# One product of ones fewer at the start, and the last subtraction of the logits moved behind h in two turns

## The chip, the cores and the metric

The kernel runs on one core of one Trainium2 chip. The time is device microseconds of one execution; several executions give a median. A profile of one execution is taken beside them, with the core's span (first to last instruction) and each engine's instructions. The engines are TensorE (PE; its weight loads are PEld), VectorE (DVE), ScalarE (ACT), GpSimd (POOL) and SyncE (SP, which issues most DMAs).

## The reference, cut

```python
h  = x + A_ref(layernorm(x), wqkv, w_phi, wo)   # x: 1 x 2048 x 512
h2 = h + B_ref(layernorm(h), w1, b1, w2, b2)

def A_ref(x, wqkv, w_phi, wo):                  # 32 heads of 16
    q, k, v = split_heads(x @ wqkv)
    pq, pk = q @ w_phi, k @ w_phi               # per head
    phi_q = concat(softmax(pq), softmax(-pq))   # 32 features; phi_k the same from pk
    kv, z = phi_k^T @ v, sum over s of phi_k
    o = (phi_q @ kv) / (phi_q @ z + 1e-6)
    return merge_heads(o) @ wo

def B_ref(x, w1, b1, w2, b2):                   # across the 2048 tokens
    u = gelu(x^T @ w1 + b1)                     # 512 x 1792
    return (u @ w2 + b2)^T
```

## The kernel before, in words

The 2048 tokens are 16 tiles of 128 rows. Each float32 operand is split in a high and a low part, and a product is three matmuls: high by high, high by low, low by high (`mm3`, L64 to L68). The program has these stages:

- **Opening** (0 to about 45 us). `WARM` products of a 128x128 tile of ones (L352) run on TensorE before any weight has arrived. Then the weights of q and k are centred (`center`), folded with `w_phi` and a block pattern (`fold`, L330) and split.
- **Passes over the tiles** up to about 130 us: keys, values and the first query tiles. Here only TensorE's order is written by hand; the other engines' instructions are put in order by the program's own model of time.
- **Attention stage** (about 138 to 260 us): the loop `for it in range(NT + 2)`, 18 turns, with the order of TensorE, VectorE, ScalarE and GpSimd written by hand (`manual_schedule`): each of these engines does its instructions in the order in which the code issues them. A turn `it` holds steps for several tiles:
  - TensorE: `s_num(it-1)` (L609, tile `pn`), transposes `s_tr(it)` (L591), a first piece of `work` (half a projection of a query tile, `q_half`, or a step of the first w1 product, `fill`), `s_wo(it-1)` (`po`, L66 to L68), then the rest of `work`.
  - VectorE: the logits of a query tile, in three instructions: `mx` (L169), `mn` (L170) and the subtraction `eq<-pu,mx` (L163, `shift` in `logit_ops`), which reads the projection from PSUM; between the last two `ol` (L618); the two sums `smq` of another tile (L234, `q_sum`); the six instructions of `s_den` that end in the weights `w` (L497 to L505); `s_h` (L634: `h` = `po` + x, with its row sums), whose result SyncE stores; and low parts of w1 (`wlo`, L670, in `flush`).
  - GpSimd: `s_pq` (L508), `s_rstd` (L645), `s_ez` (L484), the low part of `hn` (L62) and `negate` (L177, L178), which makes the negated half of the logits that were subtracted a turn before.
  - ScalarE: moments of `h`, `oh` (L613), `pht` (L593), the exponentials (L189), `hn`, high parts of w1 (L663).
- **MLP**: the rest of the w1 products (`pu<-hs,whi`) up to about 376 us, then the w2 products (`py`).

Three things about PSUM matter here. The query projections `PS[t]` are tiles of the pool `ps_q`, which has two buffers used in turn. Once the logits of all 16 tiles have been issued, `fill(1, ps_q)` takes its two tiles from the same pool. `pn` and `po` share one buffer of the pool `ps_n`, which `oh`, `ol` and `h` read.

Which steps a turn holds follows from counters (`q["mm"]`, `q["logits"]`, `q["exp"]`, `q["sum"]`), the halves listed in `Q_TURNS`, and the rule that sums are taken only while `q["sum"] <= it + 2`. `ql` is the list of a turn's three logit steps, or empty; `sm` that of its two sums, or empty.

Of the kernel before, what the change touches and what calls it, by code (L numbers as in the profile page):

```python
# [29 lines left out]
SUMS = 8  # L30
Q_TURNS = ((0, 1), (0, 1), (0, 1), (0, 1), (0,), (1,), (0,), (1,))
LAG = 3
WARM = 10
EPS = 1e-5


# [1 line left out]
def block_kernel(ctx: ExitStack, tc: tile.TileContext, x, xT, wT, phic, wo, w1, b1, w2, b2,  # L38
# [134 lines left out]
    def negate():  # L173

        if MN:
            ev, mx, mn = MN.pop(0)
            nc.gpsimd.tensor_sub(mn, mn, mx)  # L177
            nc.gpsimd.tensor_sub(ev[:, :, 1], mn.unsqueeze(3).to_broadcast([P, NPR, 2, DH]), ev[:, :, 0])  # L178

    def turns(*lists):  # L180

        return [ops[i] for i in range(max(map(len, lists))) for ops in lists if i < len(ops)]

    def run(*lists):
        for op in turns(*lists):
            op()
# [56 lines left out]
    def q_logits(lag):  # L243
        n = q["logits"]
        if n < min(NT, q["mm"] - lag + NT * (q["mm"] == NT)):
            EQ[n] = big.tile([P, NG, P], F32, name="eq", tag="big")
            q["logits"] += 1
            return logit_ops(PS[n], EQ[n], n >= Q_EARLY)
        return []

    def q_exp(lag):
        n = q["exp"]
        if n < min(NT, q["logits"] - len(MN) - lag):
            exps(n, EQ[n])
            q["exp"] += 1

    def q_sums(lag):
        n = q["sum"]
        if n < min(NT, q["exp"] - lag + NT * (q["exp"] == NT)):
            q["sum"] += 1  # L260
            return q_sum(n)
        return []
# [12 lines left out]
    with tc.tile_pool(name="prep", bufs=1) as prep:  # L275
# [74 lines left out]
        warm = ps_k.tile([P, P], F32, name="pk_ps", tag="pk_ps")  # L350
        for _ in range(WARM):
            nc.tensor.matmul(warm, ones, ones, start=True, stop=True)  # L352
# [129 lines left out]
    def s_ez(t):  # L482
        EZ[t] = az.tile([P, NG, P], F32, name="ez")
        nc.gpsimd.tensor_mul(EZ[t], EQ[t], zB)  # L484
# [22 lines left out]
    def s_pq(t):  # L507
        nc.gpsimd.tensor_mul(heads(EQ[t]), heads(EQ[t]), W[t].rearrange("p g c h -> p (g c h)").unsqueeze(2).to_broadcast([P, 2 * H, DH]))  # L508
# [77 lines left out]
    def s_tr(t):  # L586
        PHT[t] = ak.tile([P, NG, P], F32, name="pht")
        ptr = ps_t.tile([P, 8, P], F32, name="tr").rearrange("p (r c) (a s) -> p r (c a) s", r=2, a=2)
        for g in range(NG):
            for r, rows in enumerate(HALF):  # L590
                nc.tensor.transpose(ptr[:, r, g, :], EQ[t][rows, g, :], ident[rows, rows])  # L591
        for r in range(2):
            nc.scalar.activation(PHT[t][:, :, r * 64:r * 64 + 64], ptr[:, r], AF.Copy)  # L593

    def s_kv():

        pt = banks("pt")[:, 0, 0:2]
        for b in range(2):
            nc.tensor.transpose(pt[:, b, :], kvS[:, 2 * b:2 * b + 2, :].rearrange("p n f -> p (n f)"), ident)
        nc.scalar.activation(kvB, pt, AF.Copy)  # L600

    def s_num(t):

        pn = banks("pn")[:, :, 0:2]
        for b in range(2):
            for c in range(4):
                for r, rows in enumerate(HALF):
                    cols = slice(32 * c, 32 * c + 32)
                    nc.tensor.matmul(pn[cols, r, b, :], kvB[rows, b, cols], PHT[t][rows, 4 * b + c, :],  # L609
                                     start=True, stop=True, skip_group_check=True)  # L610
        oh = ak.tile([P, 2, 2, P], F32R, name="oh")
        ol = ak.tile([P, 2, 2, P], F32R, name="ol")
        nc.scalar.activation(oh, pn, AF.Copy)  # L613
        OS[t] = oh, ol, pn

    def s_ol(t):
        oh, ol, pn = OS[t]
        return [lambda: nc.vector.tensor_sub(ol, pn, oh)]  # L618

    def s_wo(t):  # L620
        oh, ol, _ = OS.pop(t)
        PO[t] = po = banks("po")[:, 0].rearrange("p a s -> p (a s)")
        for j in range(4):
            mm3(po, oh[:, j // 2, j % 2, :], ol[:, j // 2, j % 2, :], woh[:, j, :], wol[:, j, :], j == 0, j == 3)

    def s_x(t):
        HT[t] = ak.tile([P, D], F32, name="h", bufs=4)
        nc.sync.dma_start(HT[t], x[t * P:(t + 1) * P, :])

    def s_h(t):  # L630

        h = HT[t]
        VE[t] = ak.tile([P, 4], F32, name="ve2", bufs=3)
        nc.vector.scalar_tensor_tensor(h, PO.pop(t), 1.0, h, op0=ALU.mult, op1=ALU.add, accum_out=VE[t][:, 2:3])  # L634
        nc.sync.dma_start(out[t * P:(t + 1) * P, :], h)

    def s_moments(t):

        junk = ak.tile([P, D], F32, name="hj", bufs=1)
        nc.scalar.activation(VE[t][:, 1:2], VE[t][:, 2:3], AF.Copy, scale=-1.0 / D)  # L640
        nc.scalar.activation(junk, HT[t], AF.Square, bias=VE[t][:, 1:2], accum_out=VE[t][:, 3:4])  # L641
        nc.scalar.activation(VE[t][:, 0:1], VE[t][:, 3:4], AF.Identity, scale=(1.0 + EPS) / D, bias=eps2)

    def s_rstd(t):
        nc.gpsimd.tensor_tensor(r2[:, t:t + 1], VE[t][:, 0:1], mhalf[:, :1], op=ALU.pow)  # L645

    def s_hn(t):
        hn = ak.tile([P, D], F32, name="hn")
        nc.scalar.activation(VE[t][:, 1:2], VE[t][:, 1:2], AF.Copy, scale=r2[:, t:t + 1])
        nc.scalar.activation(hn, HT[t], AF.Identity, scale=r2[:, t:t + 1], bias=VE[t][:, 1:2])  # L650
        HN[t] = big.tile([P, 2, D], F32R, name="hs", tag="big")
        split(HN[t][:, 0], HN[t][:, 1], hn, nc.gpsimd)
# [6 lines left out]
    def his():  # L659
        while COMING:  # L660
            LATER.append(COMING.pop(0))
            _, raw, wh_ = LATER[-1]
            nc.scalar.activation(wh_, raw, AF.Copy)  # L663

    def flush(n=None):
        if n is None:
            his()
        for _ in range(len(LATER) if n is None else min(n, len(LATER))):
            wl_, raw, wh_ = LATER.pop(0)
            LO.append(nc.vector.tensor_sub(wl_, raw, wh_).ins)  # L670
# [40 lines left out]
    def turn(it):  # L711

        halves = Q_TURNS[it] if it < len(Q_TURNS) else ()
        n = [FN[0] <= it - LAG and FN[0] < NT, min(2, max(0, it - LAG + 1 - FN[1])) if q["logits"] == NT else 0]
        for p in range(2):
            ahead = n[p] + 1 + p + 2 * (it == NT)
            if it >= (LAG - 1, len(Q_TURNS) - 1)[p] and FL[p] < min(NT, FN[p] + ahead):
                fill_load(p)
        return ([lambda i=i: q_half(i) for i in halves] + [lambda: fill(0, ps_f)] * n[0]
                + [lambda: fill(1, ps_q)] * n[1])  # L720

    for it in range(NT + 2):
        if it < NT:
            s_x(it)
        shifted = q["logits"] - len(MN)
        ql = q_logits(0)
        work = turn(it)
        if it > NT:
            his()
        if 0 <= it - 2 < NT:  # L730
            s_moments(it - 2)
        if 0 <= it - 1 < NT:
            s_num(it - 1)
        if it < NT:
            s_tr(it)
        if it + 1 < NT:
            s_pq(it + 1)
        for w in work[:1]:
            w()
        if it == 0:  # L740
            s_kv()
        if q["exp"] < shifted:
            q_exp(0)
        if 0 <= it - 2 < NT:
            s_rstd(it - 2)
        if it + 3 < NT:
            s_ez(it + 3)
        if 0 <= it - 2 < NT:
            s_hn(it - 2)
        negate()  # L750
        left = len(LATER)
        his()
        sm = q_sums(0) if q["sum"] <= it + 2 else []
        ol = s_ol(it - 1) if 0 <= it - 1 < NT else []
        run(ql[:2] + ol + ql[2:] if ql else sm[:1] + ol)
        flush(left)
        run(sm if ql else sm[1:])
        if it > 0 and it + 2 < NT:
            run(s_den(it + 2, ps_t, "tr"))
        if 0 <= it - 1 < NT:  # L760
            s_wo(it - 1)
        for w in work[1:]:
            w()
        if 0 <= it - 1 < NT:
            s_h(it - 1)
        flush(1)
    flush()
    ms.close()
# [306 lines left out]
```

## Time and profile before

| what | us |
|---|---|
| median of 3 runs | 519.4 (519.24 to 519.52) |
| the profiled execution | 519.69 |
| its span | 517.9 |
| TensorE busy | 513.2 |
| VectorE busy | 395.0 |
| ScalarE busy | 285.3 |
| GpSimd busy | 235.9 |

A busy time is the union of an engine's instructions. A line of an engine in order of time reads: start, length, engine, line, operation, what is written `<-` what is read, shapes, count, and in brackets idle time of the engine before it with what ended that. Matmuls overlap: the next one starts before the record of the last one ends, so the step from start to start is the measure. A line of the waits reads: who waited, for what, us in total, times, longest. In a line by stretches of time, the last three numbers are granted TensorE clock, DMA share and GB/s. 1.8 us of the profiled execution lie outside the span.

### The profile page before, as it was taken

The page shows a single profiled execution, that of the slowest core. Times are in us where ns is not written, and L with a number is a line of the kernel's source. Part 1 is how long each engine was busy: PE and PEld are TensorE (multiplying, and loading weights), DVE is VectorE, ACT ScalarE, POOL GpSimd, SP SyncE. Part 2 cuts the span into 40 slices and gives each one's busy share as a digit, 9 for nine tenths or more (in the row PEclk, how much of TensorE's full clock was granted, in tenths as well). Part 3 has the DMA queues.
Part 4 walks back from the last instruction along what each step waited for, and adds up shares of the span by engine and source line. Part 5 has one row for each costly group of instructions (what it writes and reads, how often), then busy time and mean ns, then how long its engine had stood idle before and what let it go on. Part 6 is the DMA issues. An engine that isn't in the chain of part 4 may idle for free.

```text
span 517.9 us, 9772 instructions
## 1 busy us (share of the span) xinstructions
PE 513.2 (99%) x3761; PEld 434.0 (84%) x3761; DVE 395.0 (76%) x719; ACT 285.3 (55%) x501; POOL 235.9 (46%) x182
## 2 busy tenths in 40 slices
PE   9999999999999999999999999999999999999997
PEld 8888888888887777777788888888899999999997
DVE  6799889989987899697336624625797899888993
ACT  6999853526267877767756423425464434433530
POOL 3579997876999999974224000000001102110210
PEclk9999999999999999999999999999999999999999
DMA  8642301021302334333255433532134586557732
GB/s 311 209 142 84 102 22 42 1 83 44 122 27 97 103 103 119 107 103 123 82 163 162 123 94 90 184 102 62 41 115 94 141 201 136 139 156 181 137 48 61
DMA packets 46493, 57.66 MB, mean 111 GB/s; under 512 B 4080, under 2 KB 33136, under 8 KB 46448
## 3 DMA queue, kind: packets, MB, share of 16 engines
q1 hardware_dynamic: 43136, 51.38, 31.4%
q0 software_dynamic: 3024, 5.51, 7.6%
q8 instruction: 29, 0.48, 0.4%
q10 hardware_dynamic: 288, 0.17, 0.1%
q14 instruction: 16, 0.13, 0.1%
HBM read 46.81 MB, written 10.22 MB: 110 GB/s over the span
## 4 chain that ended last, share of the span: by engine, by line
PE 97%; DVE 1%; ACT 1%; issue 0%; DVEq 0%
PE pu L66 13%; PE pu L68 12%; PE pu L67 12%; PE py L921 11%; PE py L913 10%; PE py L924 6%; PE po L66 3%; PE pk_ps L66 3%; PE po L68 3%; PE po L67 3%; PE pk_ps L67 3%; PE pk_ps L68 3%; PE pv L67 3%; PE pv L66 3%; PE pv L68 3%; PE tr L591 2%
## 5 line engine op out<-in xcount | busy, mean ns | idle before, releaser
L991 POOL DMA_DIRECT2D out<-ot x14 | 12.5, 941 | 170.3 <-DVE ot L972 170.3
L66 PE MATMUL pu<-hs,whi 128*128 128x512 f32 x224 | 87.7, 394 | 0.0
L67 PE MATMUL pu<-hs,whi 128*128 128x512 f32 x224 | 87.2, 389 | 0.0
L68 PE MATMUL pu<-hs,wlo 128*128 128x512 f32 x224 | 86.5, 389 | 0.0
L670 DVE TENSOR_TENSOR wlo<-wraw,whi 128x512 fp32r<-128x512 f32 x56 | 46.9, 841 | 46.5 <-ACT whi L663 46.2
L875 ACT ACTIVATE whi<-wraw 128x1792 fp32r<-128x1792 f32 x26 | 44.0, 1704 | 30.9 <-issue 17.4
L663 ACT ACTIVATE whi<-wraw 128x512 fp32r<-128x512 f32 x56 | 34.6, 625 | 44.4 <-PE pu L67 39.4
L875 DVE TENSOR_TENSOR wlo<-wraw,whi 128x1792 fp32r<-128x1792 f32 x26 | 52.4, 2019 | 0.0
L66 PEld LDWEIGHTS pu<-hs,whi 128*128 128x128 f32 x224 | 42.0, 188 | 9.1 <-ACT hj L641 0.2
L68 PEld LDWEIGHTS pu<-hs,wlo 128*128 128x128 f32 x224 | 42.0, 188 | 8.9
L67 PEld LDWEIGHTS pu<-hs,whi 128*128 128x128 f32 x224 | 42.1, 188 | 8.5
L921 PE MATMUL py<-uf,whi 128*128 128x512 f32 x175 | 48.4, 395 | 0.0
L484 POOL TENSOR_TENSOR ez<-eq,zB 128x1024 f32<-128x1024 f32 x16 | 38.4, 2405 | 3.8 <-ACT zB L544 3.8
L913 PE MATMUL py<-uf,whi 128*128 128x256 f32 x210 | 39.0, 283 | 0.0
L213 POOL TENSOR_TENSOR pk<-pk,sk 128x1024 f32<-128x1024 f32 x16 | 31.1, 1949 | 11.2 <-DVE sk L212 10.0
L508 POOL TENSOR_TENSOR eq<-eq,w 128x1024 f32<-128x1024 f32 x16 | 32.4, 2026 | 3.2 <-DVE w L505 3.2
L921 PEld LDWEIGHTS py<-uf,whi 128*128 128x128 f32 x175 | 30.1, 189 | 3.9
L913 PEld LDWEIGHTS py<-uf,whi 128*128 128x128 f32 x210 | 32.8, 192 | 0.0
L217 POOL TENSOR_TENSOR zacc<-zacc,pk 128x1024 f32<-128x1024 f32 x13 | 31.4, 2412 | 0.5
L924 PEld LDWEIGHTS py<-uf,wlo 128*128 128x128 f32 x175 | 27.1, 189 | 3.8
L913 PE MATMUL py<-uf,wlo 128*128 128x256 f32 x105 | 29.7, 283 | 0.0
L924 PE MATMUL py<-uf,wlo 128*128 128x256 f32 x175 | 28.7, 281 | 0.0
(200 smaller groups left out, 1303.9 us busy)
## 6 DMA issues: line engine op xcount, KB each, us to landing
wraw<-in_w SPq DMA_DIRECT2D x112, 256.0 KB, 3.0
xraw<-in_xT SPq DMA_DIRECT2D x16, 256.0 KB, 2.9
xh<-in_x SPq DMA_DIRECT2D x16, 256.0 KB, 2.6
h<-in_x SPq DMA_DIRECT2D x16, 256.0 KB, 2.7
out<-h SPq DMA_DIRECT2D x16, 256.0 KB, 2.1
out<-ot POOLq DMA_DIRECT2D x14, 256.0 KB, 4.4
wraw<-in_wT SPq DMA_DIRECT2D x12, 256.0 KB, 5.1
out<-low POOLq DMA_DIRECT2D x7, 256.0 KB, 4.2
```

The lines of the kernel that those rows point to most:

```text
L66: nc.tensor.matmul(o, ah, bh, start=first, stop=False)
L67: nc.tensor.matmul(o, ah, bl, start=False, stop=False)
L68: return nc.tensor.matmul(o, al, bh, start=False, stop=last).ins
L217: nc.gpsimd.tensor_add(zacc, zacc, PK[t])
L484: nc.gpsimd.tensor_mul(EZ[t], EQ[t], zB)
L508: nc.gpsimd.tensor_mul(heads(EQ[t]), heads(EQ[t]), W[t].rearrange("p g c h -> p (g c h)").unsqueeze(2).to_broadcast([P, 2 * H, DH]))
L663: nc.scalar.activation(wh_, raw, AF.Copy)
L670: LO.append(nc.vector.tensor_sub(wl_, raw, wh_).ins)
L875: in_order(lambda: nc.scalar.activation(wh_, raw, AF.Copy), lambda: nc.vector.tensor_sub(wl_, raw, wh_))
L913: in_order(lambda: nc.tensor.matmul(o, x[:, m[0]], UB[p, m[1]][:, y], start=opens and p == 0 and i == 0, stop=closes and p == NP - 1 and i ...
L921: in_order(lambda: nc.tensor.matmul(o, wh_[:, m[0]], UB[p, m[1]], start=p == 0, stop=False, skip_group_check=True))
L924: in_order(lambda: nc.tensor.matmul(o[:, 0], wl_[:, m[0]], UB[p, m[1]][:, 0], start=False, stop=p == NP - 1, skip_group_check=True))
```

## The change

`WARM` becomes 9 instead of 10. In the attention loop a turn that holds both logits and sums issues the last of its three logit steps (the subtraction L163, and the note for `negate` of the next turn) behind `s_h` instead of behind `ol`; other turns stay as they are.

```diff
-WARM = 10
+WARM = 9
...
         sm = q_sums(0) if q["sum"] <= it + 2 else []
         ol = s_ol(it - 1) if 0 <= it - 1 < NT else []
-        run(ql[:2] + ol + ql[2:] if ql else sm[:1] + ol)
+        late = ql[2:] if sm else []
+        run(ql[:2] + ol + (ql[2:] if not late else []) if ql else sm[:1] + ol)
         flush(left)
         run(sm if ql else sm[1:])
...
         for w in work[1:]:
             w()
         if 0 <= it - 1 < NT:
             s_h(it - 1)
+        run(late)
         flush(1)
```

## The prediction

> **What bounds the kernel now.** I read the page first, then the waits, then the stretch that the change touches, engine by engine in order of time.
>
> ```profile
> span 517.9 us, 9772 instructions
> PE 513.2 (99%) x3761; PEld 434.0 (84%) x3761; DVE 395.0 (76%) x719; ACT 285.3 (55%) x501; POOL 235.9 (46%) x182
> ...
> PE 97%; DVE 1%; ACT 1%; issue 0%; DVEq 0%
> ```
>
> The first two lines are the span and the busy times, the last is the chain that ended last. TensorE is busy in 513.2 of 517.9 us and makes up 97% of the chain. So the question for each edit is only this: when does the next matmul start? Work that another engine does sooner is worth nothing unless a matmul was waiting for it, and a new wait of TensorE is paid in full, since there is hardly an idle moment later on to take it back.
>
> The waits between 140 and 260 us (the attention stage) hold only these two of TensorE for VectorE (total, times, longest):
>
> ```profile
> PEld po L66 <- DVE ol L618: 0.9, 3, 0.4
> PE pn L609 <- DVE h L634: 0.2, 1, 0.2
> ```
>
> **Where the change acts.** In a turn the loop issues VectorE's work in a fixed order. The sums are taken only once tile `q["sum"]` is not above turn + 2, the logits only while tiles are left. Counting the four counters through the opening list of passes (six query tiles done there, ten projected before turn 0, the halves of `Q_TURNS` after) gives logits in turns 0 to 4, 6 and 8, and sums from turn 5 on. So `late` holds something in two turns, 6 (tile 14) and 8 (tile 15, the last). The trace agrees: a maximum `mx` and the sums `smq` stand in one turn only at 177 to 185 and at 193 to 200 us.
>
> **Turn 6, what is removed.** The two ends of the same step are VectorE's rows and TensorE's:
>
> ```profile
> 179.77 0.69 DVE L618 TENSOR_TENSOR ol<-pn,oh 128x512 fp32r<-128x512 f32 x1 [0.76 <-ACT oh L613]
> 180.37 0.68 DVE L163 TENSOR_TENSOR eq<-pu,mx 128x512 f32<-128x512 f32 x1
> 180.97 1.27 DVE L234 TENSOR_REDUCE smq<-eq 128x32 f32<-128x512 f32 x2
> ...
> 184.71 0.68 DVE L634 SCALAR_TENSOR_TENSOR h<-po,h 128x512 f32<-128x512 f32 x1
> ...
> 185.32 1.54 DVE L670 TENSOR_TENSOR wlo<-wraw,whi 128x512 fp32r<-128x512 f32 x1
> ```
>
> ```profile
> 178.04 0.39 PE L68 MATMUL pu<-hs,wlo 128*128 128x512 f32 x1
> 178.36 0.67 PE L609 MATMUL pn<-pht,kvB 64*32 64x128 f32 x32
> ...
> 183.58 0.39 PE L68 MATMUL po<-woh,ol 128*128 128x512 f32 x1
> ...
> 184.94 0.39 PE L68 MATMUL pu<-hs,wlo 128*128 128x512 f32 x1
> 185.55 0.67 PE L609 MATMUL pn<-pht,kvB 64*32 64x128 f32 x32 [0.22 <-DVE h L634]
> ```
>
> From 179.77 on VectorE never pauses; the subtraction `eq<-pu,mx` holds it for 0.60 us (180.37 to 180.97). `pn` of the next turn needs the bank that `h` reads. Its usual step behind the last matmul is 0.32 us (178.04 to 178.36); here it is 0.61. So `h` being late costs 0.29 us. With the subtraction behind it `h` starts at 184.11, its operand `po` being done by about 184.0 (183.58 plus 0.39). It ends 0.6 us sooner, and the wait of 0.29 us goes. Next to be late is nothing of VectorE's: `wlo` starts at 185.32 as before, since the same instructions have run without a pause.
>
> How much of the 0.29 lasts? Only as far as turn 8, where TensorE meets VectorE again. VectorE's own time gains less:
>
> ```profile
> 190.97 0.22 DVE L505 TENSOR_TENSOR w<-smq,tr 128x64 f32<-128x64 f32 x1
> 191.22 0.69 DVE L634 SCALAR_TENSOR_TENSOR h<-po,h 128x512 f32<-128x512 f32 x1
> ...
> 193.26 0.68 DVE L169 TENSOR_REDUCE mx<-pu 128x32 f32<-128x512 f32 x1
> ...
> 194.46 0.68 DVE L618 TENSOR_TENSOR ol<-pn,oh 128x512 fp32r<-128x512 f32 x1
> 195.06 0.68 DVE L163 TENSOR_TENSOR eq<-pu,mx 128x512 f32<-128x512 f32 x1
> 195.66 1.26 DVE L234 TENSOR_REDUCE smq<-eq 128x32 f32<-128x512 f32 x2
> ...
> 199.25 0.22 DVE L505 TENSOR_TENSOR w<-smq,tr 128x64 f32<-128x64 f32 x1
> 199.39 0.68 DVE L634 SCALAR_TENSOR_TENSOR h<-po,h 128x512 f32<-128x512 f32 x1
> ...
> 200.00 1.19 DVE L670 TENSOR_TENSOR wlo<-wraw,whi 128x512 fp32r<-128x512 f32 x1
> ```
>
> In turn 8, where VectorE is the late one, `h` follows 0.14 us behind the start of `w`; in turn 7 it is 0.25. TensorE coming sooner can save VectorE that 0.1 us and no more, after which all is back to back until 200 us.
>
> **Turn 8, what is added.** The subtraction also does something else: it is the last reader of the PSUM bank that holds tile 15's query projection. That pool (`ps_q`, two buffers) is handed on in turn: tile 14, tile 15, then the two `pu` tiles of the second pair of w1 columns, which `fill(1, ps_q)` opens in the first turn in which all 16 tiles have their logits. That is turn 8, the same turn, behind `po`:
>
> ```profile
> 195.19 0.49 PE L66 MATMUL po<-woh,oh 128*128 128x512 f32 x1
> 195.53 0.40 PE L67 MATMUL po<-wol,oh 128*128 128x512 f32 x1
> ...
> 197.80 0.39 PE L68 MATMUL po<-woh,ol 128*128 128x512 f32 x1
> 198.03 0.39 PE L66 MATMUL pu<-hs,whi 128*128 128x512 f32 x1
> ...
> 198.71 0.39 PE L66 MATMUL pu<-hs,whi 128*128 128x512 f32 x1
> 198.94 0.39 PE L67 MATMUL pu<-hs,whi 128*128 128x512 f32 x1
> ...
> 200.84 0.67 PE L609 MATMUL pn<-pht,kvB 64*32 64x128 f32 x32
> ```
>
> The three matmuls from 198.03 open the first of the two (tile 14's old bank, free since turn 6); those from 198.71 the second, in tile 15's bank. Before, that bank is free at 195.74 (195.06 plus 0.68), 3 us ahead. After, VectorE does sums and weights 0.60 us sooner, `h` at 198.79, and the subtraction 0.61 us behind it (199.39 to 200.00 is that step), at 199.40 to 200.08; less the 0.1 us of turn 7, 199.98. A weight load follows such an end by 0.05 us (`ol` ends at 195.14, `po` starts at 195.19), so the matmul of 198.71 starts at 200.03: 1.32 us later. Behind a wait the first step is 0.34 us (195.19 to 195.53) instead of 0.23 (198.71 to 198.94): 0.11 more. **Together 1.43 us**, which already contains turn 6's gain, because VectorE's time sets it and not TensorE's. Had only TensorE's earlier arrival counted, the 0.29 would be used up in the same wait.
>
> Queued behind the waiting load on TensorE are eight more matmuls of `fill(1)`, then `pn` and the transposes of turn 9; ScalarE's `oh`, VectorE's `ol` and the next `po` wait for `pn`. All of it moves by 1.43 us. From 200 us on only the two short waits for `ol` of the table above (under 0.9 us with the one at 195.19) could give some back: at most 0.2 us, taken as nothing. On the other engines the move costs nothing. VectorE: `wlo` behind it starts when it did before, and its weights are wanted turns later. GpSimd: the negated half is taken at 192.75 and 207.52 us, 7 us behind the subtraction. SyncE: the store of `h` is issued 0.6 us sooner, with no one behind it waiting.
>
> ```profile
> 192.75 0.70 POOL L177 TENSOR_TENSOR mn<-mn,mx 128x32 f32<-128x32 f32 x1
> ...
> 207.52 0.70 POOL L177 TENSOR_TENSOR mn<-mn,mx 128x32 f32<-128x32 f32 x1
> ```
>
> **The opening.** One product of ones is two matmul records (20 for ten).
>
> ```profile
> 4.54 0.78 DVE L322 TENSOR_SCALAR wraw<-wraw,mu 128x256 f32<-128x256 f32 x2
> ...
> 4.62 1.06 PE L352 MATMUL pk_ps<-ones 128*128 128x128 f32 x4
> 5.48 2.16 PE L330 MATMUL pu<-ph,wraw 128*128 128x128 f32 x16
> 7.47 1.84 PE L330 MATMUL pv<-ph,wraw 128*128 128x128 f32 x15
> ```
>
> ```profile
> 7.63 1.79 PE pv L330 x16
> ...
> 0.00:5.00 5.00, 3.95 (x18) 3.95 (x19) 1.49 (x7) 2.00 (x3) 1.25 (x5) 1.00 0.66 191
> ```
>
> Four records lie between 4.62 and 5.48: 0.215 us each, so two are 0.43 us, the most that can be gained. The least is nothing, and I take 0.1. The first fold needs the first half of the centred weights, which VectorE finishes at 4.93 or somewhat later (half of 0.78 behind 4.54), and a weight load in front. A matmul of this shape takes 0.215 here and 0.112 in the later folds (1.79 over 16, from the chain): TensorE runs at half speed at first, although the granted clock of the first 5 us (third number from the end of the last line) reads 1.00. From 5.48 to 7.47 us 16 take 1.99 us, about two of them slow, so full speed comes at about 5.9 us; the folds that start sooner run at half speed until then, and half of what is gained is lost again. The Trainium skill ("TensorE: Matmul & The Clock Gate", Part 1, "What's actually happening") says that the array's clock starts at half and is let go after a busy window of about 3.4 us of free-running time, whatever the number of matmuls. By that the opening can't gain its full 0.43; the doubled spacing agrees, while the window itself isn't seen here.
>
> **Sum.** 1.43 less 0.10 is +1.33 us. The profiled execution took 519.69 us (517.9 span and 1.8 around it) and would take 521.0; the median of 519.4 becomes **520.7**. A difference of 0.2% (1.04 us) is about what can be told from no change.
>
> **Rivals.** (1) *The second `fill(1)` tile doesn't wait for the subtraction* (its bank is another, or the reader that frees it comes before): then what remains is a gain of 0.1 (turn 7) to 0.29 and of 0.1 at the opening, 519.0 to 519.2, not slower. For it: no wait is recorded at 198.71 now. Against it: with 3 us of lead there would be none, and two buffers leave no other bank. The point that decides is whether that matmul starts before 199.4. Chance 0.12. (2) *Both tiles wait*, if the pair's release is asked for at the first: TensorE stands from 198.03, that is 0.68 more, 521.4. Against it: three matmuls can write a bank that has been free for a dozen us. Chance 0.06. (3) *The clock is let go later*: with a product fewer the stream of ones ends at 5.05, and a pause before the folds could spoil the busy stretch. If half to all of the 30 fast folds then take 0.215 instead of 0.112, that is 1.5 to 3.1 us more, 522.2 to 523.8. The skill's window of 3.4 us at half speed would make it 1.7. Against it: the pause is under 0.2 us. Chance 0.05. (4) *The engines that the program orders by its own model before 130 us come out in another order*, since the opening is shorter: a late VectorE step of 0.68 us in a stretch without gaps, 521.4. Chance 0.02. The forecast keeps 0.75.
>
> **Range.** The forecast's own: the opening's gain at 0.43, 0.2 taken back later and 0.15 for the spread of a median give 520.0; no gain at the opening and the same spread give 521.0. Upwards rivals 2 and 4 belong in, so 520.0 to 521.6; rivals 1 and 3 (0.17) stay out. Faster by over 0.2% would need more than the 0.72 us that all gains make together: 0.02. Within 0.2% lie rival 1 and the low end of the forecast, 0.10 of its 0.75: 0.21. Slower: 0.77.
>
> **What would show it.** Right: `mx` and `smq` in turn 6 with `eq<-pu,mx` behind `h`; no wait of `pn` near 185; a new wait of TensorE for VectorE's `eq` of about 1.5 us near 199 to 200; `pn` of turn 9 at 202.2 instead of 200.84; folds starting 0.1 to 0.2 us sooner. Wrong: `pn` of turn 9 at or before 200.8 (rival 1), a wait at the first of the two tiles (2), folds spaced 0.215 us beyond 6 us (3), or new gaps of TensorE before 130 us (4).

## The result and the profile after

The changed kernel takes 521.04 us (median of 8 runs, 520.85 to 521.86), the kernel before 519.81 in its 8 runs beside it (519.24 to 520.22). The ratio is 1.0028, 95% interval 1.0017 to 1.0039: slower by 0.9 to 2.0 us. By the medians it is 1.23 us longer; +1.33 us and 520.7 were forecast. The profiled execution took 521.05 us (forecast 521.0), with a span of 519.3.

The page after, span and busy times:

```profile
span 519.3 us, 9771 instructions
PE 513.5 (99%) x3759; PEld 433.5 (83%) x3759; DVE 397.0 (76%) x719; ACT 284.8 (55%) x501; POOL 235.6 (45%) x182
```

The span grows by 1.4 us and TensorE's busy time by 0.3: the rest is new idle time. The waits between 140 and 260 us say where (who waited, for what; us in total, times, longest):

```profile
PEld pu L66 <- DVE eq L163: 1.7, 1, 1.7
PEld po L66 <- DVE ol L618: 1.5, 5, 0.4
...
PE pu L66 <- DVE eq L163: 1.3, 1, 1.3
```

The wait of `pn` for `h` is gone. One new wait stands in its place, for the moved subtraction (its weight load and its matmul each have a line), and the short waits of `po` for `ol` are five instead of three. VectorE in turns 6 to 8 and TensorE in turn 8, in order of time:

```profile
183.87 0.68 DVE L634 SCALAR_TENSOR_TENSOR h<-po,h 128x512 f32<-128x512 f32 x1
...
184.48 0.69 DVE L163 TENSOR_TENSOR eq<-pu,mx 128x512 f32<-128x512 f32 x1
185.08 1.55 DVE L670 TENSOR_TENSOR wlo<-wraw,whi 128x512 fp32r<-128x512 f32 x1
...
190.93 0.69 DVE L634 SCALAR_TENSOR_TENSOR h<-po,h 128x512 f32<-128x512 f32 x1
...
191.54 1.57 DVE L670 TENSOR_TENSOR wlo<-wraw,whi 128x512 fp32r<-128x512 f32 x1
193.03 0.68 DVE L169 TENSOR_REDUCE mx<-pu 128x32 f32<-128x512 f32 x1
...
198.56 0.68 DVE L634 SCALAR_TENSOR_TENSOR h<-po,h 128x512 f32<-128x512 f32 x1
...
199.17 0.69 DVE L163 TENSOR_TENSOR eq<-pu,mx 128x512 f32<-128x512 f32 x1
```

```profile
197.81 0.39 PE L66 MATMUL pu<-hs,whi 128*128 128x512 f32 x1
198.04 0.39 PE L67 MATMUL pu<-hs,whi 128*128 128x512 f32 x1
198.27 0.39 PE L68 MATMUL pu<-hs,wlo 128*128 128x512 f32 x1
199.91 0.50 PE L66 MATMUL pu<-hs,whi 128*128 128x512 f32 x1 [1.25 <-DVE eq L163]
200.24 0.39 PE L67 MATMUL pu<-hs,whi 128*128 128x512 f32 x1
```

Three matmuls fill the bank that had been free, and the fourth starts 0.05 us after the subtraction's end at 199.86. Its step behind the three is 1.64 us (198.27 to 199.91) instead of 0.23.

The opening:

```profile
1.05 4.21 PE L352 MATMUL pk_ps<-ones 128*128 128x128 f32 x18 [1.05 <-DVE eps L57]
5.05 2.33 PE L330 MATMUL pu<-ph,wraw 128*128 128x128 f32 x16
7.22 1.96 PE L330 MATMUL pv<-ph,wraw 128*128 128x128 f32 x16
8.94 1.23 PE L137 MATMUL pk_ps<-wkh,xs 128*128 128x256 f32 x6
```

The folds start 0.43 us sooner (5.05 against 5.48), the first projection 0.24 (8.94 against 9.18 in the profile before).

### The profile page after: what moved, and what is told of

The parts are those of the page before. It is cut to its first block, busy times and chain, and to the rows that moved or that the text cites. A ratio compares the mean times of both kernels' runs of the same rounds, so it can differ in the third digit from the quotient of the medians.

```text
span 519.3 us, 9771 instructions
## 1 busy us (share of the span) xinstructions
PE 513.5 (99%) x3759; PEld 433.5 (83%) x3759; DVE 397.0 (76%) x719; ACT 284.8 (55%) x501; POOL 235.6 (45%) x182
## 4 chain that ended last, share of the span: by engine, by line
PE 97%; DVE 1%; ACT 1%; issue 0%; DVEq 0%
PE pu L66 13%; PE pu L67 12%; PE pu L68 12%; PE py L923 11%; PE py L915 10%; PE py L926 6%; PE po L66 3%; PE pk_ps L66 3%; PE po L68 3%; PE po L67 3%; PE pk_ps L67 3%; PE pk_ps L68 3%; PE pv L66 3%; PE pv L67 3%; PE pv L68 3%; PE tr L591 2%
## 5 line engine op out<-in xcount | busy, mean ns | idle before, releaser
L670 DVE TENSOR_TENSOR wlo<-wraw,whi 128x512 fp32r<-128x512 f32 x56 | 49.5, 889 | 46.5 <-ACT whi L663 46.2
```

## The experiments

One number matters throughout: the start of a landmark on TensorE in each kernel's profile against the profile before. *Opening* is that difference at `pn` of turn 6 (from the first projection to there it moves by at most 0.06 us), *stage* what is added from `pn` of turn 6 to `pn` of turn 16, *rest* what is added from there to the end. The times in the last column are medians of 5 to 11 runs against the runs of the kernel before that were made beside them.

```
kernel                               opening  stage   rest    time against before (95%)
the change                            -0.24   +1.56  +0.04    1.0028 (1.0017 to 1.0039)
e1   nine products only               -0.18   +0.06  +0.01    1.0000 (0.9991 to 1.0009)
e2   both moves, ten products          0.00   +1.52  -0.01    1.0026 (1.0017 to 1.0036)
e3   move in turn 6, ten products     +0.49   -0.03  +0.18    1.0012 (1.0003 to 1.0021)
e10  the same once more               -0.11   +0.03  +0.18    1.0005 (0.9996 to 1.0013)
e4   move in turn 8, ten products     +0.55   +1.53  +0.19    1.0034 (1.0021 to 1.0048)
e5   the change, six ahead            -0.36   +1.42  +0.01    1.0024 (1.0013 to 1.0035)
e6   the change, ahead of h           +0.28   +1.43  -0.02    1.0034 (1.0021 to 1.0047)
e9   e5, and wlo later in turn 9      -0.28   +1.23   0.00    1.0026 (1.0017 to 1.0035)
e7   move in turn 6, ol sooner        +0.25   -0.27  +0.21    0.9997 (0.9988 to 1.0006)
e8   move in turn 6, nine products    -0.28    0.00  +0.20    1.0005 (0.9996 to 1.0014)
e11  eight products only              -0.20   +0.02  -0.02    0.9993 (0.9984 to 1.0002)
```

The stage repeats to a few hundredths; the opening differs by up to 0.66 us between executions, also where its instructions are the same (before, e2, e3, e10, e4). So the stage's share is read from the profiles and not from the medians.

The rest is 0.18 to 0.21 in five kernels and near 0 in the others. The five (e3, e10, e4, e7, e8) are those that move the subtraction in one turn only. All of it arises in one place among the w2 products, near 412 us: VectorE pauses for 0.44 us ahead of an `ot`, and a microsecond later TensorE's weight loads pause for 0.2. In e8:

```profile
410.57 0.48 DVE L974 SCALAR_TENSOR_TENSOR ot<-py,b2s,u 128x256 f32<-128x256 f32 x1 [0.44 <-DVE u L978]
```

```profile
411.84 0.19 PEld L923 LDWEIGHTS py<-un,whi 128*128 128x128 f32 x1 [0.21 <-issue]
```

The instructions there and their order are the same in all kernels, the profile names no other engine that was waited for, and no run was made to find the cause: it stays open. It lies 150 us behind the stage, so the stage's figures are free of it, but the times in the last column are not.

The theory: TensorE waits for the PSUM bank that the moved subtraction of turn 8 reads last. Rivals: the loss is made in the opening; or VectorE's changed order costs as such.

**The parts one by one: e1, e2, e3, e4.**

```diff
 e1, against before:      -WARM = 10
                          +WARM = 9
 e2, against the change:  -WARM = 9
                          +WARM = 10
 e3, as e2, and:          -late = ql[2:] if sm else []
                          +late = ql[2:] if sm and q["logits"] < NT else []
 e4, as e2, and:          -late = ql[2:] if sm else []
                          +late = ql[2:] if sm and q["logits"] == NT else []
```

> Only the opening: nine products of ones, the turns as before. Theory (the bank): the opening is a small gain of its own. In the changed kernel's profile the first projection starts 0.24 us sooner than before (8.94 against 9.18 us), so -0.1 to -0.4 us against before, no new wait of TensorE in the attention stage, and pn near 185 us still waits 0.2 us for h. Rival (the opening): the longer time of the changed kernel comes from the opening, for example full clock later; then this kernel alone is 1.2 to 1.5 us slower than before.

> Only the moved subtraction, in both turns, with ten products of ones. Theory (the bank): the whole loss and a little more than in the changed kernel, since the opening's gain is missing: +1.5 us (1.25 to 1.8). TensorE waits 1.2 to 1.3 us for VectorE's subtraction before the second tile of fill(1). Rival (the opening): 0 to -0.3 us, as before.

> The subtraction moved in turn 6 alone, ten products of ones. Theory: pn near 185 us starts 0.29 us sooner than before; turn 7's po then waits for ol, and turn 8's po again, so that the gain is given back by 196 us: 0 to -0.1 us over all. Rival (the gain lasts): -0.3 us, and po of turn 8 starts 0.29 us sooner than before.

> The subtraction moved in turn 8 alone, ten products of ones. Theory (the bank): +1.5 us (1.25 to 1.8), the same as with both turns, with TensorE's wait of 1.2 to 1.3 us for the subtraction; pn near 185 us waits 0.2 us as before. Rival (VectorE's order as such, the loss being shared by the two turns or coming from longer low parts behind the moved step): about half of the loss of both turns, 0.7 us.

The stage adds up: 1.52 with both moves, 1.53 with turn 8 alone, -0.03 with turn 6 alone, 0.06 with neither. All of the loss is turn 8's, and the two rivals fall: the opening alone does not slow the kernel, and the loss is not shared between the turns. By their medians e2 and e4 take 1.55 and 1.79 us more than before, inside the 1.25 to 1.8 expected. In e4 the wait stands by itself, beside the old one of `pn` (waits between 176 and 204 us):

```profile
PE pu L66 <- DVE eq L163: 1.2, 1, 1.2
...
PE pn L609 <- DVE h L634: 0.2, 1, 0.2
```

e1 by its runs can't be told from before, where -0.1 to -0.4 us were expected; its profile shows the opening 0.18 us shorter. The median of e3 missed its expectation: +0.7 us where 0 to -0.1 was expected, and no loss in the stage. Its profile shows the opening 0.49 us later: the folds begin at 5.48 as before, but 16 of them take 2.50 us (to 7.98) instead of 1.99, because full speed came later in that execution: the step from matmul to matmul falls from 0.21 to 0.11 us at 6.97 us there, at 5.91 before. Another 0.18 us is the rest's.

```profile
5.48 2.66 PE L330 MATMUL pu<-ph,wraw 128*128 128x128 f32 x16
7.98 1.95 PE L330 MATMUL pv<-ph,wraw 128*128 128x128 f32 x16
```

**e10, e3 once more.**

> The same kernel as the one that moves the subtraction in turn 6 alone with ten products, run once more, because its time came out 0.7 us above before while its attention stage showed no loss. Theory (the opening of those executions was late: full clock from 6.96 us in its profile): the stage again within 0.1 us of before, and the time within 0.3 us of before when the opening is. Rival (something in this kernel costs 0.5 to 0.7 us every time): +0.5 to +0.7 us again.

Stage +0.03, time 520.00 against 519.82, interval 0.9996 to 1.0013. The +0.7 us did not come back; the 0.18 us that is left is as large as the rest in its profile. That the other 0.5 us lay in the openings of the first series is shown for the one profiled execution only (0.49 us), not for the other ten.

**More cover in front of the wait: e5.** In turn 8 both steps of `fill(1)` write the first tile before either writes the second:

```diff
+    def fill_pair(p, pool):
...
+        for c in range(2):
+            for t in range(2):
+                DONE[0] = mm3(PU[p][c], a[:, t, c * P:(c + 1) * P], b[:, t, c * P:(c + 1) * P],
+                              HN[t][:, 0], HN[t][:, 1], t == 0, False)
...
-                + [lambda: fill(1, ps_q)] * n[1])
+                + ([lambda: fill_pair(1, ps_q)] if n[1] == 2 and FN[1] == 0 else [lambda: fill(1, ps_q)] * n[1]))
```

> The changed kernel, but in turn 8 the first two steps of fill(1) write their first tile twice before the second is opened: six matmuls instead of three lie ahead of the one that waits for the bank; same matmuls, same sums. Theory (the bank): TensorE's wait for the subtraction falls from 1.25 us by three matmuls of 0.227, 0.68 us, to about 0.57; the stage from turn 6's pn to turn 10's pn, which is 1.58 us longer in the changed kernel than before, becomes 0.9 longer. Rival (the loss is not that wait but VectorE's or GpSimd's later work in turns 8 and 9): the stage stays 1.5 us longer.

**The subtraction sooner: e6.**

```diff
         if 0 <= it - 1 < NT:
+            if q["logits"] == NT:
+                run(late)
+                late = []
             s_h(it - 1)
         run(late)
```

> The changed kernel, but in turn 8 the moved subtraction stands just ahead of h, behind the weights, instead of behind h. Theory (the bank): the subtraction ends about 0.62 us sooner (199.24 instead of 199.86 in the changed kernel's profile), TensorE waits 0.6 us instead of 1.25, and the stage is 0.95 us longer than before instead of 1.58. h ends where it ended before and costs nothing, since pn of turn 9 comes later. Rival (moving it off its old place costs the same wherever it goes): 1.5 us.

Both did to the wait what the theory said. TensorE in e5 and in e6:

```profile
199.78 0.50 PE L66 MATMUL pu<-hs,whi 128*128 128x512 f32 x1 [0.58 <-DVE eq L163]
```

```profile
199.83 0.50 PE L66 MATMUL pu<-hs,whi 128*128 128x512 f32 x1 [0.63 <-DVE eq L163]
```

0.58 against the 0.57 expected, and 0.63 against 0.6, where the change has 1.25. From `pn` of turn 6 to `pn` of turn 9 the loss falls from 1.58 us to 0.89 and 0.97. But the stage did not stay there: at `pn` of turn 10, where e5's expectation had 0.9 us, both stand at about 1.17, by turn 11 at 1.64, by turn 16 at 1.42 and 1.43. Of the 0.65 us taken off the wait, 0.14 are left. e5's TensorE shows where the remainder went:

```profile
209.94 0.67 PE L609 MATMUL pn<-pht,kvB 64*32 64x128 f32 x32 [0.22 <-DVE h L634]
212.99 0.50 PE L66 MATMUL po<-woh,oh 128*128 128x512 f32 x1 [0.16 <-DVE ol L618]
```

VectorE is late in turns 9 and 10, and one instruction makes it so. In turn 9, the low part of a w1 block behind `ol`, beside GpSimd's `ez`, in e5:

```profile
202.77 0.69 DVE L618 TENSOR_TENSOR ol<-pn,oh 128x512 fp32r<-128x512 f32 x1 [1.38 <-ACT oh L613]
203.38 2.65 DVE L670 TENSOR_TENSOR wlo<-wraw,whi 128x512 fp32r<-128x512 f32 x1
205.95 0.68 DVE L234 TENSOR_REDUCE smq<-eq 128x32 f32<-128x512 f32 x1
```

```profile
203.07 2.41 POOL L484 TENSOR_TENSOR ez<-eq,zB 128x1024 f32<-128x1024 f32 x1
```

`wlo` ends at 206.03, 0.55 us after `ez` (205.48); in e6 it takes 2.58 us in the same place. Before the change the same instruction came at 202.85, ahead of `ez` and beside a shorter one of GpSimd, and took its plain 0.68:

```profile
202.85 0.68 DVE L670 TENSOR_TENSOR wlo<-wraw,whi 128x512 fp32r<-128x512 f32 x1
```

```profile
202.94 1.00 POOL L645 TENSOR_TENSOR r<-ve,mhalf 128x1 f32<-128x1 f32 x1
203.91 2.41 POOL L484 TENSOR_TENSOR ez<-eq,zB 128x1024 f32<-128x1024 f32 x1
```

There GpSimd's instruction was the one that grew: `r` takes 1.00 us, and 0.54 in e5, where `wlo` is not beside it. GpSimd runs through this stretch without a pause, while `ol`, and `wlo` behind it, wait for `pn` of turn 9. So a delay of TensorE in turn 8 moves `wlo` from ahead of `ez` to beside it: in e5 `wlo` starts 0.53 us later than before and `ez` 0.84 sooner. In the change itself it is there too:

```profile
204.19 1.96 DVE L670 TENSOR_TENSOR wlo<-wraw,whi 128x512 fp32r<-128x512 f32 x1
```

There TensorE is so late already (1.58 us at `pn` of turn 9) that VectorE's 1.3 us more cost it next to nothing (1.64 at turn 11). The Trainium skill ("SBUF — State Buffer", "Who interferes with whom") says that a VectorE instruction with two SBUF inputs and a GpSimd instruction that reads SBUF contend for a read interface, and whoever comes second waits for the whole of the first. The trace agrees: `wlo`, with two SBUF inputs, ends 0.55 us behind `ez` in e5 (203.38 to 206.03) and 0.54 behind it in the change (`ez` there runs from 203.21 to 205.61, `wlo` to 206.15).

**The meeting taken away: e9.** e5, and in turn 9 `flush(left)` behind `s_den` instead of ahead of the sums:

```diff
-        flush(left)
+        if it != 9:
+            flush(left)
         run(sm if ql else sm[1:])
         if it > 0 and it + 2 < NT:
             run(s_den(it + 2, ps_t, "tr"))
+        if it == 9:
+            flush(left)
```

> The kernel with six matmuls ahead of the waiting one, and in turn 9 the low part wlo goes from behind ol to behind the weights of s_den. In that kernel TensorE's wait for the subtraction fell to 0.6 us as the theory said, but the stage ended 1.4 us longer all the same: in turn 9 wlo came to lie beside GpSimd's ez, took 2.65 us instead of 0.68, and TensorE then waited for h (0.28 us at pn of turn 10) and for ol (0.47 us at po of turn 10). Theory (a second wait behind the first, made by that meeting): without it pn of turn 10 and po of turn 10 don't wait, and from pn of turn 6 to pn of turn 12 the stage is 0.9 to 1.1 us longer than before instead of 1.6. Rival (the time is lost whatever stands there, since the bank's late release delays all of VectorE): 1.4 to 1.6 us.

`wlo` takes 0.89 us, `pn` and `po` of turn 10 wait no more, and from `pn` of turn 6 to `pn` of turn 12 the stage is 1.23 us longer than before; e5 has 1.61 there. That is above the 0.9 to 1.1 expected: in its new place `wlo` is late for the matmul that reads it, and this costs most of the other 0.35 us (`pn` of turn 9 stands at 0.88, of turn 10 at 1.23).

```profile
206.60 0.89 DVE L670 TENSOR_TENSOR wlo<-wraw,whi 128x512 fp32r<-128x512 f32 x1
```

```profile
PE pu L66 <- DVE eq L163: 0.5, 1, 0.5
PEld pu L68 <- DVE wlo L670: 0.5, 1, 0.5
```

So the second wait exists and is made by that meeting. By their medians e5, e6, e9 and the change can't be told apart: all intervals overlap. No run kept the subtraction late and gave the tile another bank, so what the late subtraction costs without any wait at that bank is not shown.

**Keeping turn 6's gain: e7, with e8 beside it.** Both move the subtraction in turn 6 alone (as e3, with nine products). e7 also takes `ol` sooner, since `po` waited for it:

```diff
-        late = ql[2:] if sm else []
-        run(ql[:2] + ol + ...
+        late = ql[2:] if sm and q["logits"] < NT else []
+        if it == 7:
+            run(ol + sm[:1])
+        elif it == 8:
+            run(ql[:1] + ol + ql[1:])
+        else:
+            run(ql[:2] + ol + ...
```

> A version that should beat both: nine products of ones, the subtraction moved in turn 6 alone, and ol taken ahead of the first sum in turn 7 and ahead of mn in turn 8, so that po no longer waits for it there. Theory (turn 6's gain is given back because po waits for ol in turns 7 and 8): turn 6's 0.29 us lasts and the 0.1 us of turn 8's po comes on top; the stage from pn of turn 6 to pn of turn 10 is 0.3 to 0.4 us shorter than before, the whole 0.3 to 0.6 us. Rival (VectorE's backlog comes back in another place): stage within 0.1 us of before.

> The changed kernel with the subtraction of turn 8 put back: nine products of ones, moved in turn 6 alone. Theory: the stage as before within 0.1 us (as turn 6 alone with ten products had it), the whole 0 to -0.2 us. It also tells whether the 0.7 us by which turn 6 alone with ten products came out slower belongs to the move or to the opening of those executions: its stage showed no loss, so the rival (the move in turn 6 costs 0.5 to 0.7 us somewhere behind the stage) wants +0.5 us here too, outside the opening.

e8's stage is as before (0.00): turn 6's 0.29 us is all given back by `pn` of turn 9. In e7 it is kept. The stage is 0.39 us shorter up to turn 12 and, with 0.12 lost again at a wait of `po` for `ol` in turn 12, 0.27 at the end. The time is 519.66 against 519.86, where 0.3 to 0.6 us less were expected; the interval (0.9988 to 1.0006) has 1 in it, so e7 beats the change but is not shown to beat the kernel before. By its profile the stage's 0.27 us are nearly all lost again in the rest (0.21), whose cause is open.

**One product fewer still: e11.** `WARM = 8`, turns as before.

> Eight products of ones, the turns as before. Theory (the first fold waits for its centred weights at about 5.0 to 5.1 us, so that only the first product fewer has something to gain): no further gain, within 0.2 us of nine products, with the first fold at 5.0 to 5.2 us and a short pause of TensorE before it. Rival (each product fewer gains its 0.43 us): first fold at 4.6 us and another 0.2 to 0.4 us off.

The folds start at 5.13 us behind a pause, as with nine products (5.13 in e1); the opening is 0.20 us shorter, against 0.18, and the intervals of the two overlap. No further gain is shown, as expected.

```profile
5.13 2.02 PE L330 MATMUL pu<-ph,wraw 128*128 128x128 f32 x16 [0.32 <-POOL ph L355]
```

The profile puts the pause down to `ph`, the pattern that GpSimd makes. But `ph` ends at 4.88 us, and the first half of the centred weights at 5.03 (VectorE, 4.51 to 5.03), 0.07 us ahead of the weight load at 5.10 that takes them. The later of the two fits, which is what was expected; but the two end 0.14 to 0.16 us apart in every run, so no run tells them apart.

## Why the prediction was right, point by point

The mechanism was the one forecast: a single new wait in turn 8, for the bank that the moved subtraction reads last. How near the sum came is partly luck. By the profiles it is 1.56 less 0.24 and 0.04 more, 1.36 us, against 1.33: the stage was put 0.13 us too small and the opening's gain 0.14 too small, and the two cancel.

- **Turn 8's wait** was the forecast's main term, 1.43 us for the stage, and the stage measured 1.56 in the change, 1.52 and 1.53 in e2 and e4. The matmul was to start at 200.03 and does at 199.91, which is 200.15 once the opening's 0.24 is added. The step from the subtraction's end (0.05 us) and the restart (0.33 against 0.34) were as read. The 0.13 us that the term was too small come from the next point.
- **What VectorE saves by turn 6's gain** was put at 0.1 us and is nothing. `h` of turn 7 came 0.05 us sooner than the opening alone makes it (191.22 less 0.24 is 190.98, measured 190.93), and `wlo` behind it took 1.57 us instead of 1.51. `mx` of turn 8 is where it was: 193.03 against 193.02.
- **Turn 6's wait** went as forecast (`pn` 0.29 us sooner in e3 and e10) and was used up before turn 9. The forecast had it last as far as turn 8 and said that nothing else of VectorE's would be late. That step was wrong: in e8 and e10, where turn 8 is as before, 0.22 and 0.25 us of it are gone by `pn` of turn 8, because `po` now waits for `ol` in turn 7 too (two such waits of 0.7 us together between 176 and 204 us, one of 0.3 before). In e7, with `ol` sooner, 0.28 is still there at `pn` of turn 8. The sum did not suffer, since turn 8's wait would have used it up.
- **The opening** was put at 0.10 us inside bounds of 0 and 0.43. Measured 0.18 and 0.24, so mis-sized, since the folds could start at 5.05 and 5.13 us and not only at about 5.3: the weight load that stands ahead of them runs beside the last product of ones (from 4.92 us in the change, where that product's record lasts to 5.26). Half of the gain is lost again to the half-speed clock, as was said.
- **"On the other engines the move costs nothing"** was wrong as a statement about turns 9 and 10: VectorE's `wlo` grew from 0.68 to 1.96 us there. It was hidden by the larger wait, so the sum did not suffer; e5, e6 and e9 show that a smaller wait would not have brought a smaller loss in proportion. The prediction's own rows could have warned of it: `wlo` takes 1.19 and 1.54 us there, against 0.68 at 202.85 in the same profile.
- **Rivals.** The second tile did wait (1), the first did not (2). The clock was not let go later because of the missing product (3): with nine products the trace's clock record has full speed from 5.8, 5.8, 4.8, 6.8, 6.6, 4.0 and 4.9 us after the span's start (the change, e1, e5, e6, e7, e8, e9), with eight 4.6 (e11), with ten from 5.9, 4.4, 7.0, 5.3 and 5.7 (before, e2, e3, e4, e10). The ranges lie over one another, and wherever matmuls run at those times their step falls from 0.21 to 0.11 us there. The order of the other engines' instructions is the same but for the moved ones (4).

## What to carry to other kernels

A step that is moved behind other work takes with it the release of what it reads: before moving a reader, find the next user of its buffer, above all at a change of stage, where another kind of work inherits the bank in the same turn. The same move was harmless in turn 6, where the bank's next user came a turn and a half later. And a wait that is shortened may uncover the next one: follow the landmarks some turns on before believing the gain.

## What the runs showed of the hardware

Full TensorE speed came between 4.0 and 7.0 us after the span's start in the thirteen profiled executions, whose first matmul always started at 1.05 or 1.06 us, and moved the opening by up to half a microsecond (e3 against before, both with folds from 5.48). The Trainium skill ("TensorE: Matmul & The Clock Gate", Part 1, "What's actually happening") calls the window free-running, so that the point depends on where in it the first matmul falls; this agrees, but its 500 ns either way from run to run are less than the 3 us seen here. It is not the only thing that moves the opening. In e4 full speed came at 5.3 us, sooner than before, and the opening is 0.55 us longer: there TensorE stood idle for 0.55 us until ScalarE had centred a block of weights, and ScalarE had waited 1.74 us for that block's DMA instead of 0.63.

```profile
8.81 1.16 PE L330 MATMUL pv<-ph,wraw 128*128 128x128 f32 x8 [0.55 <-ACT wraw L324]
```

The meeting of `wlo` and `ez`, 0.68 us against 1.96 and 2.65, had not been expected either.
